# A fifth chunk place, two swapped places and an earlier third row block in a linear-attention and Fourier mixing kernel

## The chip, the cores and the metric

The kernel runs on one core of one Trainium2 chip. The metric is the device time of one execution in microseconds (us). The kernel before takes 724.97 us, the median of three runs (724.33 to 727.36).

A core has a matrix engine (TensorE, PE in the profile, with its weight loads as PEld), a vector engine (VectorE, DVE), an engine for pointwise functions (ScalarE, ACT), and GpSimd (POOL) and SyncE (SP), which here only issue DMAs once the start is over. Each engine works through its own queue in order. They meet through semaphores. TensorE writes to banks of an accumulation memory (PSUM). Everything else lies in the on-chip memory (SBUF) or in the chip's main memory (HBM).

## The reference

The input x is 2048 x 576. The result is a gated mix of a linear attention block with 32 heads and a two-dimensional Fourier layer:

```
g = sigmoid((x * gate_w).sum(-1))
q, k, v = x @ wqkv                      # each 2048 x 576, 32 heads of 18
phi(t)  = where(t > 0, t + 1, exp(t)) + 1e-6
kv  = phi(k)^T v per head;  z = sum of phi(k) over the rows
o   = (phi(q) kv) / (phi(q) z + 1e-6)
a   = o @ wo
b   = dft_seq_re @ (x @ dft_hid_re^T) - dft_seq_im @ (x @ dft_hid_im^T)
result = g * a + (1 - g) * b
```

All is float32. The kernel keeps that precision by splitting each operand of a matmul into a high part and a low part (high on ScalarE as a rounding copy, low on VectorE as the difference), and by three matmuls for each product: high x high, high x low, low x high.

## The kernel before

The stages come one after the other, and the time of each is in the profile below.

**The k stage.** k' = phi(x W_k) is made, 16 blocks of 128 rows, and kept split on the chip (`pk`). While that runs, POOL fetches transposed blocks of x for later, two 128-row blocks (a "pair") at a time. A pair is turned into seven combined blocks ("forms"), because the products x W_q and x W_hidden are later done by a scheme of seven products for four. The class `Left` holds such a pair: its loads (line 366), sums (199), high parts (179) and low parts (189), and its stores to HBM (`xm<-xb`, line 398). Pairs 2, 3, 4 and 5 take turns in two places of SBUF of 14,336 bytes per partition, one from offset 15104 of the slot area to 29440, one from 29440 to 43776. Pair k+2 waits until pair k's stores have landed.

**The k'^T x stage** (line 752). Instead of k'^T v the kernel makes G = x^T k', and then, for each 128 rows of G, multiplies with W_v (`kv_step`). x comes as 20 chunks of 128 x 512, which I number 0 to 19: four for each of the five column blocks c. Chunk n is used in step n: 24 matmuls, or 16 in the last four steps, whose column block is narrow. A chunk is loaded by SP (`craw<-in_xg_dram`, line 599), split by ScalarE (`c<-craw`, 179) and VectorE (`c<-craw,c`, 189), and then read by TensorE. The chunks lie in a ring of four places (`cs_ring`). `xg_load` is called once per step after that step's matmuls, so the load of chunk n+4 goes into the place of chunk n; SP holds it until the matmuls of step n are done. `xg_next` splits chunk n+2 in step n.

In the same steps lies work for the q stage: the forms of pairs 6 and 8 (pair 8 stands for the odd columns of all pairs), pair 5's stores, and W_q. W_q is prepared by `right_here` in three pieces: two pieces of 128 rows (generators `wq_pieces[0]` and `[1]`, called `a` and `b` in the table `turn`) and the remaining 64 rows, laid out as 96 (`wq_pieces[2]`, `c`). Each piece is two loads by POOL (line 469), four sums on VectorE (199), one high part on ScalarE and one or two low parts on VectorE. The table `turn` says in which step a generator is moved one stage on. The second piece lies at offset 16128 to 32256 of the slot area, so it overlaps both places of the pairs. The third has its result at 32256 to 40320 and its raw data from 40320 to 48384, so it overlaps only the upper place.

**The q stage** (line 928). q' = phi(x W_q) by the seven products, in 56 slots, `q_slot`, four groups of two pairs: (6, 2), (3, 4), (0, 5), (7, 1). Some pairs' forms come from HBM (`xf<-xm`), some are made on the spot (`xb`). In the table `plan` each slot is given further work: the product of kv with W_o (`build_m`, then moved by DMA to other partitions with `move_m`, `mw<-mf`, and split with `split_m`), the forms of pairs 7, 0 and 1 (`left[k]`), the norms, and the first transposes of q' (`transposed(0)`).

**The rest.** o @ W_o (line 209 with `mw`), the hidden Fourier transforms (1133) and the two sequence transforms (1289), from 198 us on.

What sets the order: TensorE's order in the q stage, and SP's everywhere, is the order of the program text. In the k'^T x stage a scheduler orders TensorE's and POOL's instructions by a simulated timeline and by priority, so that TensorE's queue there has some matmuls of a later chunk in front of the rest of an earlier one. `pace()` fixes ScalarE's and VectorE's order to the program's.

The scratch for the exponentials, `es` (three places of 1184 bytes at `Y_AT`), is used in the k stage and in the q stage, and lies unused in between.

Of the kernel before, what the change touches and what calls it, by code (L numbers as in the profile page):

```python
# [136 lines left out]
def kernel(  # L137
# [373 lines left out]
    def go(gen, n=1):  # L511
        for _ in range(n):
            next(gen, None)
# [46 lines left out]
    for h in range(2):  # L560
        ps = [bank()[:, :QH[h]] for _ in range(FT)]
        parts = wkt.split(h, KC)
        for c, (raw, hi, lo) in enumerate(first):
            if h == 0:
                if c == 0:
                    nc.vector.tensor_copy(out=hi, in_=raw)
                else:
                    done.append(hi_of(hi, raw))
                lo_of(lo, raw, hi)
            next(parts)  # L570
            passes = ((hi, c), (lo, c), (hi, 5 + c))[:3 if c < KC else 2]
            for n, (x, j) in enumerate(passes):
                for i in range(FT):
                    nc.tensor.matmul(ps[i], x[:, i * P:(i + 1) * P], wkt.row(h, j),
                                     start=(c == 0 and n == 0), stop=(c == KC and n == 1))
        if h == 0:
            banks = ps
            lefts.append(Left(2, SLOT_AT + 15104, done[-1]).make())
    for i in range(FT):
        k_feature(i, 0, banks[i])  # L580
    split_next()
# [1 line left out]
    for i in range(FT):  # L583
        k_feature(i, 1, ps[i])
        if i < 2:
# [2 lines left out]
    wq_w, wq_pieces = right_here(wq, wq_rest, (T_AT + 112896, SLOT_AT + 16128),  # L588
                                 SLOT_AT + 32256, SLOT_AT + 40320)
    cs_ring = Ring(C_AT, 2 * CU * P * 4, 4)  # L590
    xg_order = [(c, q) for c in range(5) for q in range(NCU)]
    xg_raw, xg_split = [], []

# [19 lines left out]
    for i in range(FT, NT):  # L613
        xs = split.pop(0)
        k_half(i, 0, xs)
        if i < NT - 2:
            split_next()
        left_part()
        if i >= NT - 2:
            xg_next()  # L620
        held = pending[:]
        pending.clear()
        k_half(i, 1, xs)
        for f in held:
            f()
        if i in (10, 12, 14):
            add(zacc, zacc if i > 10 else acc[0], acc[i // 2 - 4])
        if i == 5:
            go(wq_pieces[0])
        if 8 <= i < 12:  # L630
            xg_load()
        if i < NT - 1:
            load_next()
        if i == FT:
            load_next()
        for k, j in ((3, 4), (4, 9), (5, 13)):
            if i == j:
                lefts.append(Left(k, SLOT_AT + 15104 + k % 2 * 14336, done[-1]).make())
    tick()
    nc.scalar.activation(gate, gate, AF.Exp, scale=-1.0)  # L640
    nc.vector.tensor_scalar(gate, gate, 1.0, None, op0=ALU.add)
# [77 lines left out]
    def load_two(*places):  # L719
        for p, o in places:  # L720
            forms[p] = at(o, [P, 7, 2, 2 * P], R, "xf")
        for a, b in ((2, 4), (0, 2), (4, 7)):
# [1 line left out]
                nc.sync.dma_start(out=forms[p].bitcast(F)[:, a:b], in_=xforms[p][:, a:b])  # L724

    turns = dict(p=rest_forms(), a=wq_pieces[0], b=wq_pieces[1], c=wq_pieces[2], x=left_of(6, False))
    turn = {4: "p", 5: "p", 6: "p", 7: "p", 8: "pap", 9: "pa", 10: "pax", 11: "pxpaa",
            12: "pbbxb", 13: "xcb", 14: "cc", 15: "xc", 17: "b"}

    plan = {  # L730
        2: [lambda: begin_left(NP, ACC_AT)],
        6: [z_chain, lambda: begin_left(6, ACC_AT + 22784)],
        8: [z_sum],
        12: [lambda: load_wo(2)],
        14: [lambda: load_forms(2, ACC_AT + 8448, nc.gpsimd), lambda: load_wo(3)],
# [7 lines left out]
    for c in range(5):  # L743
        ps = [bank(), bank()]
        passes = FULL if c < KC else FULL[:2]
        for q in range(NCU):
# [26 lines left out]
            del spaced[:n]  # L773
            if step == 9:
                go(wq_pieces[1])
                go(wq_pieces[2])
            for k in turn.get(step, ""):
                go(turns[k])
            step += 1
# [242 lines left out]
        44: [lambda: here[7].store(slice(0, 4), done[-1]),  # L1022
             lambda: here[7].store(slice(4, 7), done[-1])],
    }
    for k, what in ((7, (10, 11, 13, 15, 20)), (0, (13, 15, 18, 20, 20)),
                    (1, (31, 35, 36, 36, 36)), (None, (25, 27, 30, 41, 43, 45, 48, 48, 49, 52)),
                    ("m", (28, 30, 28, 35, 33))):
        for n, j in enumerate(what):
            f = norm if k is None else m_parts[n] if k == "m" else lambda k=k: go(left[k])
            plan.setdefault(j, []).append(f)  # L1030
# [10 lines left out]
    with tc.manual_schedule(engines={mybir.EngineType.PE}):  # L1041
        for k, (n, s, q) in enumerate(slots):
            q_slot(n, s, q)
            for f in plan.get(k, ()):
                f()
            if k == 49:
                nxt = transposed(0)
    while feats or dves:
        if feats:
# [465 lines left out]
```

## Time and profile before

| what | us |
|---|---|
| median of the runs (3) | 724.97 |
| profiled execution | 726.96 |
| its span, first to last instruction | 725.2 |
| TensorE busy | 716.6 |
| VectorE busy | 595.3 |
| ScalarE busy | 331.2 |

By stages, from the view of busy time in windows: from 53 to 135 us, where the k stage ends and the k'^T x stage runs, TensorE is busy all but some 3 us; from 135 to 198 (the q stage) all but about 0.6; and from 198 to 544 it has no gap in that view. How to read it: a matmul's end is modelled, so the start of the next one tells better than its end whether TensorE stood still. A row of the timeline gives start, duration, engine, line, operation, what is written from what, how many instructions are merged in the row, and in brackets the idle time before the first of them and what ended it. A row of waits gives the total, the number and the longest. In rows of DMAs the last number is the median from issue to landing. A releaser is inferred; where several semaphores are waited for, the named one is the last by the profile.

### The profile page before, as it was taken

The numbers are of one execution on the slowest core, as the hardware profiler recorded it, in microseconds if no ns is written. First come the engines' busy times: TensorE is split into PE (matmuls) and PEld (weight loads), VectorE is DVE, ScalarE is ACT, GpSimd is POOL, SyncE is SP. The second block draws the span as 40 slices with busy tenths as digits, with TensorE's granted clock in tenths as the row PEclk, the third lists the DMA queues.
The fourth block names the chain that finished last, engine by engine and source line by source line (L and its number), as shares of the span: only waits on it lengthen the run. The fifth ranks groups of instructions, "written<-read, shape, count | busy, mean of one in ns | idle before, by whom it ended". The sixth has DMA issues, their size and how long they took to land.

```text
span 725.2 us, 13800 instructions
## 1 busy us (share of the span) xinstructions
PE 716.6 (99%) x5390; PEld 714.2 (98%) x5390; DVE 595.3 (82%) x993; ACT 331.2 (46%) x507; POOL 78.7 (11%) x141
## 2 busy tenths in 40 slices
PE   9999999999999999999999999999999999999998
PEld 9999999999999999999999999999999999999997
DVE  5799987477999748989899989857889988788884
ACT  6898445478545634453334333323535322232321
POOL 1122431123252100000000000000000000000000
PEclk9999999999999999999999999999999999999999
DMA  7385789999279648444476666889963544454440
GB/s 256 117 254 188 249 277 323 328 318 271 105 274 393 247 159 320 131 163 139 153 234 203 231 224 197 281 318 398 372 210 132 172 147 127 131 171 154 153 153 33
DMA packets 54093, 157.85 MB, mean 218 GB/s; under 512 B 6884, under 2 KB 9348, under 8 KB 54028
## 3 DMA queue, kind: packets, MB, share of 16 engines
q1 hardware_dynamic: 42524, 117.23, 48.3%
q0 software_dynamic: 11216, 39.32, 15.5%
q8 instruction: 43, 0.70, 0.4%
q10 hardware_dynamic: 288, 0.41, 0.2%
q14 instruction: 22, 0.18, 0.1%
HBM read 117.80 MB, written 36.49 MB: 213 GB/s over the span
## 4 chain that ended last, share of the span: by engine, by line
PE 75%; DVE 5%; DMA 3%; ACT 2%; issue 1%; POOL 0%; DVEq 0%; POOLq 0%; ACTq 0%
PE bank L1289 49%; PE bank L1133 14%; PE bank L209 8%; PE bank L928 2%; DMA craw<-in_xg_dram 1%; PE bank L839 1%; DMA wraw<-in_wq_rest_dram 1%; DVE xb L189 1%; ACT xb L179 1%; DMA xb<-in_xq_dram 1%; DVE sum L199 1%; PE bank L752 1%; DVE acc L938 0%; DVE den L808 0%; DVE xb L199 0%
## 5 line engine op out<-in xcount | busy, mean ns | idle before, releaser
L1289 PE MATMUL bank<-fh,c 128*128 128x288 f32 x1792 | 355.8, 295 | 0.0
L1289 PEld LDWEIGHTS bank<-fh,c 128*128 128x128 f32 x1792 | 285.9, 188 | 0.2 <-DVE c L189 0.2
L1289 PE MATMUL bank<-fl,c 128*128 128x288 f32 x896 | 262.8, 293 | 0.0
L179 ACT ACTIVATE c<-craw 128x1792 fp32r<-128x1792 f32 (+1 forms) x84 | 121.4, 1447 | 185.5 <-DVE craw L199 162.5
L1289 PEld LDWEIGHTS bank<-fl,c 128*128 128x128 f32 x896 | 168.7, 188 | 0.0
L189 DVE TENSOR_TENSOR c<-craw,c 128x1792 fp32r<-128x1792 f32 (+4 forms) x86 | 141.9, 1653 | 4.7 <-ACT c L179 4.5
L199 DVE TENSOR_TENSOR craw<-craw 128x256 f32<-128x256 f32 (+1 forms) x192 | 98.1, 512 | 21.6 <-DMA craw<-in_ci_dram 10.8
L1133 PE MATMUL bank<-wf,xf 128*128 128x288 f32 x630 | 98.5, 296 | 0.0
L1133 PEld LDWEIGHTS bank<-wf,xf 128*128 128x128 f32 x630 | 90.0, 189 | 0.0
L752 PE MATMUL bank<-pk,c 128*128 128x288 f32 x448 | 62.4, 297 | 3.2 <-DVE c L189 1.8
L752 PEld LDWEIGHTS bank<-pk,c 128*128 128x128 f32 x448 | 60.2, 188 | 4.1 <-DVE c L189 2.5
L209 PE MATMUL bank<-mw,qs 128*128 128x288 f32 x448 | 63.2, 297 | 0.1
L209 PEld LDWEIGHTS bank<-mw,qs 128*128 128x128 f32 x448 | 59.9, 188 | 0.6 <-ACT qs L179 0.4
L209 PE MATMUL bank<-wd,xs 128*128 128x288 f32 (+1 forms) x336 | 44.7, 295 | 0.0
L209 PEld LDWEIGHTS bank<-wd,xs 128*128 128x128 f32 x336 | 44.6, 188 | 0.0
L199 DVE TENSOR_TENSOR ys<-bank,ys 128x288 f32<-128x288 f32 x63 | 28.8, 456 | 17.4 <-PE bank L1289 14.2
L189 DVE TENSOR_TENSOR fl<-fl,fh 128x864 fp32r<-128x864 f32 (+1 forms) x32 | 34.6, 1092 | 7.0 <-ACT fh L179 5.8
L179 ACT ACTIVATE fh<-fl 128x864 fp32r<-128x864 f32 (+1 forms) x32 | 29.8, 950 | 16.3 <-DVE fl L199 16.3
L398 POOL DMA_DIRECT2D xm<-xb x56 | 30.3, 547 | 29.0 <-ACT sum L969 8.4
L1133 PE MATMUL bank<-wf,xr 96*128 96x288 f32 x112 | 33.3, 298 | 0.0
L1311 ACT ACTIVATE ys<-bank 128x288 f32<-128x288 f32 x16 | 6.6, 413 | 56.3 <-PE bank L1289 56.3
L199 DVE TENSOR_TENSOR ys<-ys,bank 128x288 f32<-128x288 f32 x47 | 21.1, 449 | 13.3 <-PE bank L1289 12.7
(133 smaller groups left out, 805.1 us busy)
## 6 DMA issues: line engine op xcount, KB each, us to landing
xf<-xm SPq DMA_DIRECT2D x49, 512.0 KB, 9.2
craw<-in_cr_dram SPq DMA_DIRECT2D x32, 512.0 KB, 3.6
craw<-in_ci_dram SPq DMA_DIRECT2D x32, 512.0 KB, 3.8
xm<-xb POOLq DMA_DIRECT2D x56, 256.0 KB, 4.7
xr<-xr SPq DMA_DIRECT2D x21, 448.0 KB, 8.7
craw<-in_xg_dram SPq DMA_DIRECT2D x20, 256.0 KB, 5.7
att<-acc POOLq DMA_DIRECT2D x16, 288.0 KB, 3.2
row<-att SPq DMA_DIRECT2D x16, 288.0 KB, 4.3
```

The costliest lines, as they stand in the source:

```text
L179: return nc.scalar.activation(dst, src, AF.Copy, bias=bias)
L189: nc.vector.tensor_tensor(out=dst, in0=src, in1=hi, op=ALU.subtract)
L199: nc.vector.tensor_tensor(out=dst, in0=a, in1=b, op=op)
L209: nc.tensor.matmul(ps, a, b, start=(n == 0), stop=(n == len(pairs) - 1))
L398: ins = nc.gpsimd.dma_start(out=xforms[self.k][:, f], in_=self.c.bitcast(F)[:, f])
L752: nc.tensor.matmul(ps[h][:, :HALF], t[:, a, k], pk[s][:, b, half(h)], start=(s == 0 and n == 0), stop=(s == NT - 1 and n == len(passes) - 1))
L839: nc.tensor.transpose(banks[c // KC][:, (c % KC) * P:(c % KC + 1) * P], a, ident)
L928: nc.tensor.matmul(ps, a, b, start=(start and n == 0), stop=(stop and n == len(ops) - 1), skip_group_check=True)
L1133: nc.tensor.matmul(ps, a, b, start=(start and n == 0), stop=(n == len(ops) - 1), skip_group_check=True)
L1289: nc.tensor.matmul(ps[q], c[x][:, l, k], factors[p](y, f), start=(p == 0 and i == 0), stop=(p == NP - 1 and i == 2))
L1311: nc.scalar.activation(c11, ps[1], AF.Copy)
```

## The change

Four things are changed together. First, `cs_ring` gets a fifth place at `Y_AT`, on the scratch of the exponentials: chunk n+4 now goes to the place of chunk n-1. Second, the two places of the pairs are swapped: pairs 2 and 4 now lie in the upper place, 3 and 5 in the lower. Third, W_q's third piece is loaded in step 7 (it was step 9, after the second piece) and its sums, high part and low part come in steps 10 to 12, ahead of the second piece's. Fourth, some work has other slots in the q stage: the last low part of pair 0 goes from slot 20 to 23 and that of pair 1 from 36 to 38, `split_m(0, 0)` from 28 to 24, `split_m(1, 1)` from 35 to 34, and the first transposes from after slot 49 to after slot 50.

```diff
-            lefts.append(Left(2, SLOT_AT + 15104, done[-1]).make())
+            lefts.append(Left(2, SLOT_AT + 29440, done[-1]).make())
...
     cs_ring = Ring(C_AT, 2 * CU * P * 4, 4)
+    cs_ring.at.append(Y_AT)
...
-                lefts.append(Left(k, SLOT_AT + 15104 + k % 2 * 14336, done[-1]).make())
+                lefts.append(Left(k, SLOT_AT + 29440 - k % 2 * 14336, done[-1]).make())
...
-    turn = {4: "p", 5: "p", 6: "p", 7: "p", 8: "pap", 9: "pa", 10: "pax", 11: "pxpaa",
-            12: "pbbxb", 13: "xcb", 14: "cc", 15: "xc", 17: "b"}
+    turn = {4: "p", 5: "p", 6: "p", 7: "p", 8: "pap", 9: "pa", 10: "paxc", 11: "pxpaac",
+            12: "pcxcb", 13: "xbb", 14: "b", 15: "x", 17: "b"}
...
+        7: [lambda: go(wq_pieces[2])],
...
                 go(wq_pieces[1])
-                go(wq_pieces[2])
...
-    for k, what in ((7, (10, 11, 13, 15, 20)), (0, (13, 15, 18, 20, 20)),
-                    (1, (31, 35, 36, 36, 36)), (None, (25, 27, 30, 41, 43, 45, 48, 48, 49, 52)),
-                    ("m", (28, 30, 28, 35, 33))):
+    for k, what in ((7, (10, 11, 13, 15, 20)), (0, (13, 15, 18, 20, 23)),
+                    (1, (31, 35, 36, 36, 38)), (None, (25, 27, 30, 41, 43, 45, 48, 48, 49, 52)),
+                    ("m", (24, 30, 28, 34, 33))):
...
-            if k == 49:
+            if k == 50:
                 nxt = transposed(0)
```

The order of SP's queue is the same in both kernels, and TensorE's too but for the transposes. What moves on the other engines is shown at three places. Numbers behind names only tell buffers apart.

POOL's queue in steps 6 to 9 of the k'^T x stage, before. `xm_110` are pair 4's stores, `xb_1274` pair 6's loads, `xm_111` pair 5's stores, and the loads of line 469 are W_q's second and third rows:

```order
L398 DMA xm_110<-xb_691 128x512 x7
L366 DMA xb_1274<-in_xq_dram 128x2x256 x2
L398 DMA xm_111<-xb_894 128x512 x7
L469 DMA wraw_1411<-in_wq_dram 128x3x288
L469 DMA wraw_1411<-in_wq_dram 128x288
L469 DMA wraw_1415<-in_wq_rest_dram 96x864
L469 DMA wraw_1415<-in_wq_rest_dram 96x288
```

The same place after the change:

```order
L398 DMA xm_110<-xb_691 128x512 x7
L469 DMA wraw_1313<-in_wq_rest_dram 96x864
L469 DMA wraw_1313<-in_wq_rest_dram 96x288
L366 DMA xb_1274<-in_xq_dram 128x2x256 x2
L398 DMA xm_111<-xb_894 128x512 x7
L469 DMA wraw_1415<-in_wq_dram 128x3x288
L469 DMA wraw_1415<-in_wq_dram 128x288
```

The third rows' two loads have moved past pair 6's loads and pair 5's stores; the second rows' loads are still behind those stores.

VectorE's queue from chunk 13's low part (`c_1394`) to chunk 15's (`c_1482`), before. `c_1449` is chunk 14, `wraw_1411` and `wb_1412` are W_q's second rows, `wraw_1415` the third, `xb_1275` is pair 6:

```order
L189 TENSOR_TENSOR c_1394<-craw_1392,c_1394 128x512
L189 TENSOR_TENSOR plain_1406<-wraw_1407,plain_1406 128x576
L189 TENSOR_TENSOR gt_1491<-bank,gt_1491 128x288 x2
L199 TENSOR_TENSOR wraw_1411<-wraw_1411 128x288 x4
L189 TENSOR_TENSOR c_1449<-craw_1447,c_1449 128x512
L189 TENSOR_TENSOR xb_1275<-xb_1274,xb_1275 128x4x256
L199 TENSOR_TENSOR wraw_1415<-wraw_1415 96x288 x2
L189 TENSOR_TENSOR wb_1412<-wraw_1411,wb_1412 128x4x288
L189 TENSOR_TENSOR c_1482<-craw_1480,c_1482 128x512
```

After the change, where `c_1398` is chunk 13, `c_1484` chunk 15, `wraw_1415` now the second rows and `wb_1314` the third:

```order
L189 TENSOR_TENSOR c_1398<-craw_1396,c_1398 128x512
L189 TENSOR_TENSOR plain_1410<-wraw_1411,plain_1410 128x576
L189 TENSOR_TENSOR gt_1495<-bank,gt_1495 128x288 x2
L189 TENSOR_TENSOR wb_1314<-wraw_1313,wb_1314 32x2016
L199 TENSOR_TENSOR wraw_1415<-wraw_1415 128x288 x2
L189 TENSOR_TENSOR c_1449<-craw_1447,c_1449 128x512
L189 TENSOR_TENSOR xb_1275<-xb_1274,xb_1275 128x4x256
L199 TENSOR_TENSOR wraw_1415<-wraw_1415 128x288 x2
L189 TENSOR_TENSOR c_1484<-craw_1482,c_1484 128x512
```

Ahead of chunk 14's low part stand two sums on the second rows instead of four, and the second rows' low part has gone from before chunk 15's low part to behind it; the third rows' low part has come to the front.

ScalarE's queue in slots 22 to 28 of the q stage, before. `e` are exponentials of q', `sum_1959` and `sum_1960` copies from the banks, and `mw_2241` the high parts of the product of kv with W_o:

```order
L937 ACTIVATE e_2171<-sum_1967,less_88 128x288
L937 ACTIVATE e_2183<-sum_1968,less_88 128x288
L941 ACTIVATE e_2193<-bank 128x288
L942 ACTIVATE e_2193<-e_2193 128x288
L967 ACTIVATE sum_1959<-bank 128x288
L937 ACTIVATE e_2214<-sum_1965,less_88 128x288
L967 ACTIVATE sum_1960<-bank 128x288
L179 ACTIVATE mw_2241<-mw_2085 128x1152 x2
```

After the change (`mw_2185` is the same product):

```order
L938 ACTIVATE e_2170<-sum_1967,less_88 128x288
L938 ACTIVATE e_2183<-sum_1968,less_88 128x288
L179 ACTIVATE mw_2185<-mw_2085 128x1152
L942 ACTIVATE e_2195<-bank 128x288
L943 ACTIVATE e_2195<-e_2195 128x288
L968 ACTIVATE sum_1959<-bank 128x288
L938 ACTIVATE e_2216<-sum_1965,less_88 128x288
L968 ACTIVATE sum_1960<-bank 128x288
L179 ACTIVATE mw_2185<-mw_2085 128x1152
```

One of the two high parts has moved ahead of five other instructions.

## The prediction

> **What bounds the kernel now.** I read the page first, then what TensorE's weight loads waited for, then TensorE's rows in the stage that the change touches.
>
> ```profile
> span 725.2 us, 13800 instructions
> PE 716.6 (99%) x5390; PEld 714.2 (98%) x5390; DVE 595.3 (82%) x993; ACT 331.2 (46%) x507; POOL 78.7 (11%) x141
> ...
> PEld bank L752 <- DVE c L189: 2.5, 3, 1.2
> PEld bank L752 <- ACT c L179: 1.6, 1, 1.6
> ...
> PEld bank L928 <- DVE xb L189: 0.6, 1, 0.6
> ```
>
> TensorE is busy for 99% of the span, and the change takes no matmul away. So all that can be won is idle time of TensorE: 4.1 us (2.5 + 1.6) at line 752, the stage k'^T x, and 0.6 us in the q stage (L928). Beyond that there is next to nothing to gain.
>
> ```profile
> 99.40 0.64 PE L752 MATMUL bank<-pk,c 128*128 128x288 f32 x3
> 101.37 12.51 PE L752 MATMUL bank<-pk,c 128*128 128x288 f32 x92 [1.34 <-ACT c L179]
> ...
> 114.69 0.77 PE L752 MATMUL bank<-pk,c 128*128 128x288 f32 x4
> 115.89 3.45 PE L752 MATMUL bank<-pk,c 128*128 128x288 f32 x24 [0.43 <-DVE c L189]
> 119.75 5.11 PE L752 MATMUL bank<-pk,c 128*128 128x288 f32 x36 [0.40 <-DVE c L189]
> ...
> 128.62 2.37 PE L752 MATMUL bank<-pk,c 128*128 128x288 f32 x16
> 132.00 2.44 PE L752 MATMUL bank<-pk,c 128*128 128x288 f32 x16 [1.01 <-DVE c L189]
> ```
>
> These are TensorE's rows around the four stalls. Ninety-two matmuls in 12.51 us start 0.134 us apart. After the three at 99.40 the next was due at 99.80 and came at 101.37: stall 1, 1.57 us. In the same way stall 2 is 0.66 (due 115.23), stall 3 is 0.64 (due 119.11), and stall 4 is 1.24 (due 130.76). The sum is 4.11, as the weight loads have it.
>
> **Stalls 1 and 4: the fifth place.** They come from late chunks.
>
> ```profile
> SPq L599 <- PE bank L752: 38.9, 15, 5.0
> ...
> 88.38 7.02 SPq L599 DMA_DIRECT2D craw<-in_xg_dram  x3
> 118.85 0.33 SPq L599 DMA_DIRECT2D craw<-in_xg_dram  x1
> 122.71 8.06 DMA craw<-in_xg_dram
> ...
> 97.01 0.63 ACT L179 ACTIVATE c<-craw 128x512 fp32r<-128x512 f32 x1 [0.76 <-DMA craw<-in_xg_dram]
> 100.69 0.63 ACT L179 ACTIVATE c<-craw 128x512 fp32r<-128x512 f32 x1 [3.04 <-DMA craw<-in_xg_dram]
> 130.85 0.63 ACT L179 ACTIVATE c<-craw 128x512 fp32r<-128x512 f32 x1 [5.60 <-DMA craw<-in_xg_dram]
> ```
>
> The first row says that 15 chunk loads waited for TensorE: with four places, chunk n+4 is loaded when step n is done. With five it is loaded when step n-1 is done, one step (24 x 0.134 = 3.2 us) sooner, where nothing else holds SP.
> Stall 1 waits for chunk 12's high part, 100.69 on ScalarE. Its load is the last of the three from 88.38 on, at 88.38 + 7.02 - 0.33 = 95.07, and it landed near 100.6. One step sooner is 91.9, so it lands near 97.5. ScalarE has made chunk 11's part at 97.01 + 0.63 and is free, so the part is there near 98.3, before 99.80. Stall 1 goes, with 1.5 us to spare: -1.57. Next late would be chunk 13, which no matmul needs for another three steps.
> Stall 4 waits for chunk 19, issued at 122.71 and landed 8.06 later. One step sooner is the time of the row at 118.85, less what stalls 1 and 3 give back by then (about 1.6): 117.3. Landed after the same 8.06 it is there at 125.4, split about 1.2 later on ScalarE and VectorE, and due at 130.76 - 2.2 = 128.6. Stall 4 goes too, with 2 us to spare: -1.24.
> The fifth place lies on the scratch of the exponentials in the k and q stages. Chunk 4 waits there for the k stage's last features, which end before step 0 does; chunk 19 is used up before the q stage's first features are due: 0.
>
> **Stalls 2 and 3: W_q.** These two come from VectorE's queue.
>
> ```profile
> 113.42 1.81 DVE L199 TENSOR_TENSOR wraw<-wraw 128x288 f32<-128x288 f32 x4 [4.46 <-DMA wraw<-in_wq_rest_dram]
> 115.16 0.68 DVE L189 TENSOR_TENSOR c<-craw,c 128x512 fp32r<-128x512 f32 x1
> 115.76 1.22 DVE L189 TENSOR_TENSOR xb<-xb,xb 128x1024 fp32r<-128x1024 f32 x1
> 116.89 0.93 DVE L199 TENSOR_TENSOR wraw<-wraw 96x288 f32<-96x288 f32 x2
> ...
> 119.02 0.68 DVE L189 TENSOR_TENSOR c<-craw,c 128x512 fp32r<-128x512 f32 x1
> ...
> 122.51 2.25 DVE L189 TENSOR_TENSOR wb<-wraw,wb 32x2016 fp32r<-32x2016 f32 x1 [0.75 <-ACT wb L179]
> ...
> 120.59 1.89 ACT L179 ACTIVATE wb<-wraw 96x2016 fp32r<-96x2016 f32 x1 [2.13 <-DVE wraw L199]
> ...
> 93.76 1.07 POOL L398 DMA_DIRECT2D xm<-xb  x2 [0.41 <-ACT zb L659]
> 98.06 1.08 POOL L398 DMA_DIRECT2D xm<-xb  x2 [3.22 <-ACT c L179]
> 105.33 1.31 POOL L469 DMA_DIRECT2D wraw<-in_wq_dram  x2 [6.20 <-issue]
> ...
> wraw<-in_wq_dram POOLq DMA_DIRECT2D x1, 432.0 KB, 7.2
> ```
>
> VectorE stands for 4.46 us before the sums on W_q's second rows, and chunk 14's low part (115.16 to 115.84) is queued behind all four. The row names the third rows; by the program it is the second that are summed there, issued at 105.33 and 7.2 us on the way, the small piece behind them a little more.
> After the change two sums stand ahead of chunk 14 instead of four, which saves 0.9, but TensorE comes 1.57 sooner, at 113.66. The load itself can hardly go earlier: POOL starts it when pair 5's stores have landed, and their last two go after chunk 11's high part. That part's 0.76 us of waiting for its chunk ends, so all of it moves by about 0.7: sums from 112.7, low part at 112.7 + 0.93 + 0.66 = 114.3. Stall 2 is then 0.65 and stays: 0. Bounds: unmoved load, 115.0, stall 1.35 (+0.7); a load that lands another 0.65 sooner, since the third rows no longer follow it, no stall (-0.66).
> Stall 3: between the two chunks' low parts stood xb, two sums, a low part of W_q; now only xb and two sums: 1.1 + 0.9 + 0.65 = 2.7 us after chunk 14, where TensorE needs it 24 x 0.134 = 3.2 after. It goes: -0.64. ScalarE must not be later than that; its high part of W_q's second rows (1.9 us) now stands behind chunk 15's.
> The third rows, two DMAs, now go about 89, ahead of pair 6's loads on POOL, which the swap allows: they overlap the place of pair 4 alone. Their work is covered by VectorE's wait. VectorE began it at 113.42 - 4.46 = 108.96, so 107.4 with stall 1 gone; ScalarE's high part (1.89) and then VectorE's low part (2.25) end near 111.7, a microsecond ahead of 112.7: 0. Were that cover gone, each microsecond would go into stall 2. For the swap itself, two pairs each still share a place: 0.
>
> **The q stage.** No gain is booked. The pieces that move are two low parts of 0.95 us on VectorE, one of the two W-products' high parts on ScalarE, and a transpose one product later.
>
> ```profile
> 162.21 2.06 ACT L937 ACTIVATE e<-sum,less 128x288 f32<-128x288 f32 x4 [2.06 <-DVE sum L199]
> 165.95 2.21 ACT L179 ACTIVATE mw<-mw 128x1152 fp32r<-128x1152 f32 x2
> 165.54 1.45 POOL L366 DMA_DIRECT2D xb<-in_xq_dram  x2 [10.79 <-ACT sum L967]
> ...
> 185.00:198.00 13.00, 12.85 (x99) 12.56 (x98) 12.74 (x30) 6.97 (x18) 3.57 (x7) 1.00 0.36 142
> ```
>
> From 185 to 198 VectorE (third pair of numbers) is busy 12.74 of 13 us beside a TensorE busy 12.85. Both are full there, so TensorE ends the stage when VectorE does, and VectorE's work stays the same. The chain that leads there starts at exponentials that wait 2.06 us for VectorE's sums; they release pair 1's load at 165.54. Pair 0's low part (0.95) moves behind those sums, and one high part (2.21 / 2 = 1.1) moves ahead of the release: +0.15, taken as 0. Bounds: -0.6 (L928's wait goes) to +1.1 (the low part was no help).
>
> **The sum.** -1.57 + 0 - 0.64 - 1.24 = -3.45. The profiled execution took 726.96 (span 725.2, 1.72 around it): 723.5. The median shown is 724.97, 1.99 less than that. If those 1.99 lie outside the stalls, the new median is 724.97 - 3.45 = 721.5. If the median run simply has that much less of the stalls, only 1.5 of the 3.45 is there to win: 723.5. I take the middle, 722.5.
>
> **Two rules of the Trainium skill.** The page "DMA: Bandwidth & Descriptors", section "Anatomy of one DMA — SWDGE (gpsimd) path", gives a GpSimd DMA a fixed 2.0 us plus bytes by 436 GB/s; for 432 KB that is an estimate of 3.0 us, stall 2 would vanish and the sum be -4.1. The 7.2 us of this trace disagrees. The same page, section "Issuing engines are not separate DMA queues", says that DMAs of all issuers share the same 16 engines, so starting them otherwise wins only issue time; that speaks against this change and would lead to rival C.
>
> **Rivals.**
>
> ```profile
> 125.00:135.00 10.00, 8.99 (x69) 8.76 (x69) 5.13 (x10) 2.25 (x6) 0.11 (x1) 1.00 0.96 360
> ...
> 152.88 1.25 SPq L712 DMA_DIRECT2D xr<-xr  x2
> xr<-xr SPq DMA_DIRECT2D x2, 448.0 KB, 8.7
> mw<-mf SPq DMA_DIRECT2D x1, 252.0 KB, 10.0
> ...
> 88.72 1.46 POOL L366 DMA_DIRECT2D xb<-in_xq_dram  x2 [7.15 <-ACT c L179]
> 76.89 0.72 POOL L372 DMA_DIRECT2D xb<-in_xq_dram  x1 [1.81 <-issue]
> ```
>
> A, all goes: stall 2 and the q waits end as well. 724.97 - 4.1 - 0.6 = 720.3, or some 721 if the median has less to lose. For it: the small piece only needs 0.65.
> B, given back in the q stage: ScalarE's first high part of the W-product, moved from slot 28 to 24, needs a 9 KB piece that SP issues behind two loads of xr. The second of these goes about 153.8 and takes 8.7: 162.5. ScalarE comes at 164.27 - 0.95 = 163.3, so in the old timing nothing waits; but if TensorE comes 3.45 sooner and these DMAs don't, it waits 2.6, and pair 1's load, VectorE's chain and TensorE with it. 724.97 - 3.45 + 2.7 = 724.2; with the next piece's 10.0 us, up to 726.6. Against it: these DMAs are released by TensorE's own progress, so they should move along.
> C, it doesn't do what it says: the DMA engines are 0.96 busy from 125 to 135. If chunk 19 lands at 130.8 whenever it is issued, TensorE still resumes at 132.00, and every stall won before is lost there: 725.0. Against it: chunk 19's load was among the last that went, and it now goes 5 us sooner.
> D, slower: POOL works in order. The third rows' loads go where the loads of 88.72 went, and wait for pair 4's stores; pair 6's loads, pair 5's seven stores and the second rows' load stand behind them. POOL has also waited 1.81 us at 76.89 for nothing but its own queue. If two more DMAs in flight put off the stores by one landing (4 us), the second rows are 4 us later and stall 2 is 0.65 + 4.1: 725.6. From 3.45 us of delay on it is slower than before, from 7.1 by over 0.5%: 728.6. For it: stall 2 has no slack at all. Against it: the stores at 93.76 went 4 us before the last two at 98.06, which wait for ScalarE, not for POOL.
>
> **Chances.** Forecast 0.57 (its own range 721.4 to 723.6), A 0.16, B 0.12, C 0.08, D 0.07. A difference under 0.5% (3.6 us) is about what a measurement of this kernel can't tell from none. Faster than 721.35 takes A and the edge of the forecast: 0.19. Slower than 728.6 is half of D and a little of B: 0.05. Within: 0.76. The range goes from 720.7 (most of A) to 725.5 (B's middle, C, D's edge).
>
> **What would show it.** Right: TensorE's waits at the chunk stage's matmuls fall from 4.1 to about 0.7 us, ScalarE no longer waits 3.04 and 5.60 us for chunks 12 and 19, VectorE still waits for W_q's second rows near 112, and the q stage's rows are shifted by 3 to 4 us. Wrong: a wait before the matmuls on pair 1 (L928) that is longer than 0.6 us (B), chunk 19 landing near 130 again (C), W_q's second rows issued later than 105.3 (D).

## The result and the profile after

| | median us | executions | ratio to the kernel before, 95% interval |
|---|---|---|---|
| before | 725.39 | 10 | |
| after | 722.94 | 10 | 0.9953, [0.9941, 0.9966] |

The three executions shown ahead (median 724.97) are among the ten. The median of the kernel after is 2.45 us lower, 0.34%; the ratio in the table, which is not that of the two medians, lies 0.47% below 1, and its interval excludes 1. So the kernel after is faster, by about as much as the prediction's bound of 0.5%; the median forecast was 722.5. The profiled execution of the kernel after took 724.75, the slowest of its ten (the fastest took 720.50), against 726.96 before.

The page of the kernel after, its first lines:

```profile
span 723.0 us, 13795 instructions
PE 715.7 (99%) x5390; PEld 714.7 (99%) x5390; DVE 594.8 (82%) x993; ACT 331.1 (46%) x507; POOL 79.0 (11%) x141
```

What TensorE's weight loads waited for in the kernel after (total us, times, longest). Line 754 is the stage k'^T x, which was 752 before; 929 is the q stage, which was 928:

```profile
PEld bank L754 <- DVE c L189: 1.5, 1, 1.5
PEld bank L929 <- DVE xb L189: 1.4, 1, 1.4
```

Of 4.1 us at the chunks' matmuls 1.5 is left, in one piece. Before the matmuls on pair 1 there is now 1.4 where 0.6 stood. TensorE's rows in the chunk stage of the kernel after:

```profile
100.05 12.87 PE L754 MATMUL bank<-pk,c 128*128 128x288 f32 x95
...
113.73 0.76 PE L754 MATMUL bank<-pk,c 128*128 128x288 f32 x4
115.81 8.29 PE L754 MATMUL bank<-pk,c 128*128 128x288 f32 x60 [1.31 <-DVE c L189]
124.72 2.33 PE L754 MATMUL bank<-pk,c 128*128 128x288 f32 x16
127.85 4.53 PE L754 MATMUL bank<-pk,c 128*128 128x288 f32 x32
```

Stall 1 is gone: the 95 matmuls from 100.05 on hold the three that stood alone at 99.40 and the 92 behind the stall. Stalls 3 and 4 are gone too: sixty matmuls and then thirty-two run through where rows broke off at 119.75 and 132.00. Stall 2 has grown. The fourth matmul from 113.73 on starts at 114.20, the next was due 0.134 later and came at 115.81: 1.47 us. Counted like this, from one start to the next less 0.134, the four stalls of the kernel before are 1.50, 0.60, 0.57 and 1.17, together 3.8; the prediction's 4.11 takes its due times from the starts of rows. All stalls from here on are counted from start to start, so stall 2 went from 0.60 to 1.47.

All times of this execution lie 0.64 us late from 16 us on. Its first loads are not the reason: TensorE began its first x products at 5.07 us here and at 5.25 before. But from 5.45 to 6.90 they start 0.24 us apart here, and about 0.134 apart before. The trace's record of TensorE's granted clock, the share of full speed that it is given, has its first entry at full clock at 6.95 us here and at 4.83 before; 0.24 us is also the spacing under a granted clock of 0.50 further below (no_q_slots). So the clock rose later in this execution. In a second execution of the same kernel (after_again) it rose at 4.21, so this differs from one execution to the next. By 16 us the profiled executions of this study lie up to 0.8 us apart.

ScalarE's rows for chunks 12 and 19 in the kernel after:

```profile
97.94 0.63 ACT L179 ACTIVATE c<-craw 128x512 fp32r<-128x512 f32 x1 [0.53 <-DMA craw<-in_xg_dram]
...
126.16 0.63 ACT L179 ACTIVATE c<-craw 128x512 fp32r<-128x512 f32 x1 [2.70 <-DMA craw<-in_xg_dram]
```

They stood at 100.69 and 130.85. Both chunks are now early enough.

Stall 2, first on POOL's queue and then on VectorE, in the kernel after:

```profile
97.83 1.07 POOL L398 DMA_DIRECT2D xm<-xb  x2 [1.31 <-ACT c L179]
106.06 1.31 POOL L469 DMA_DIRECT2D wraw<-in_wq_dram  x2 [7.16 <-DMA xm<-xb]
```

```profile
114.19 0.95 DVE L199 TENSOR_TENSOR wraw<-wraw 128x288 f32<-128x288 f32 x2 [2.09 <-DMA wraw<-in_wq_dram]
115.06 0.69 DVE L189 TENSOR_TENSOR c<-craw,c 128x512 fp32r<-128x512 f32 x1
```

Pair 5's last two stores go at 97.83, so 0.87 sooner than before once the 0.64 is taken off. The load that waits for their landing goes at 106.06, which is 105.42 less the 0.64: where it went before (105.33). The stores took longer. This is the DMA view of the stretch from 97 to 107.5 us, with the median us from issue to landing, of the kernel before and of the kernel after:

```profile
xm<-xb POOLq DMA_DIRECT2D x2, 256.0 KB, 5.5
```

```profile
xm<-xb POOLq DMA_DIRECT2D x2, 256.0 KB, 6.5
wraw<-in_wq_dram POOLq DMA_DIRECT2D x1, 432.0 KB, 7.3
```

And the stretch from 95 to 105, of before and of after; the last three numbers are the granted clock, the busy share of the DMA engines and the GB/s:

```profile
95.00:105.00 10.00, 8.66 (x67) 8.43 (x67) 8.54 (x17) 4.13 (x6) 1.08 (x2) 1.00 0.91 327
```

```profile
95.00:105.00 10.00, 10.00 (x79) 10.00 (x79) 9.83 (x20) 4.08 (x5) 2.35 (x5) 1.00 1.00 382
```

The share rose from 0.91 to 1.00. Whether fuller engines make these stores slow is tested below.

The q stage of the kernel after, VectorE's rows and TensorE's:

```profile
170.38 0.76 DVE L199 TENSOR_TENSOR xb<-xb 128x256 f32<-128x256 f32 x2 [2.19 <-DMA xb<-in_xq_dram]
...
175.22 1.23 DVE L189 TENSOR_TENSOR xb<-xb,xb 128x1024 fp32r<-128x1024 f32 x1 [1.27 <-ACT xb L179]
```

```profile
174.91 0.43 PE L929 MATMUL bank<-wb,xb 128*128 128x288 f32 x2
176.50 0.80 PE L929 MATMUL bank<-wb,xb 128*128 128x288 f32 x4 [1.16 <-DVE xb L189]
```

VectorE waits for pair 1's load, whose second half landed at 170.29, and TensorE resumes 6.2 us after the landing. This wait is 1.32 us, against 0.54 before. Two small gaps that the kernel before had, 0.18 at 162 and 0.29 at 197, are gone.

### The profile page after: what moved, and what is told of

It is laid out like the page before. It is cut to its first block, busy times and chain, and to the rows that moved or that the text cites. A ratio compares the mean times of both kernels' runs of the same rounds, so it can differ in the third digit from the quotient of the medians.

```text
span 723.0 us, 13795 instructions
## 1 busy us (share of the span) xinstructions
PE 715.7 (99%) x5390; PEld 714.7 (99%) x5390; DVE 594.8 (82%) x993; ACT 331.1 (46%) x507; POOL 79.0 (11%) x141
## 4 chain that ended last, share of the span: by engine, by line
PE 92%; DMA 3%; DVE 2%; ACT 1%; issue 0%; POOL 0%; DVEq 0%; POOLq 0%
PE bank L1290 49%; PE bank L209 15%; PE bank L1134 15%; PE bank L754 6%; PE bank L929 4%; PE bank L574 2%; PE bank L840 1%; DMA wraw<-in_wq_dram 1%; DMA xm<-xb 1%; DMA xb<-in_xq_dram 1%; ACT xb L179 1%; DVE xb L189 1%; PE bank L235 1%; DVE xb L199 0%; DVE sum L199 0%
```

## The experiments

The theory after this comparison: the stalls lie one behind another, and the middle one hangs on a load whose time TensorE does not set. Pair 5's last store lands; 1 us later the load of W_q's second rows goes; some 7 us later it lands; then VectorE's sums run, and chunk 14's low part behind them. Taking stall 1 away brings TensorE sooner to that same landing. The first rival is that the four terms add up one by one, as the prediction had them.

**The fifth place alone (fifth_only).** On the kernel before:

```diff
     cs_ring = Ring(C_AT, 2 * CU * P * 4, 4)
+    cs_ring.at.append(Y_AT)
```

> The kernel before with the fifth place alone. Theory (stalls are coupled: chunk 14's low part waits in VectorE's queue behind the four sums on W_q's rows, and those wait for a load whose landing does not follow TensorE): stalls 1 and 4 go (-1.57, -1.24), but TensorE only comes 1.57 us sooner to stall 2, which grows from 0.66 to about 2.2; stall 3 stays at 0.64. Net -1.2 us, 724.2. Rival (the terms simply add, as the prediction had them, and the load of the second rows moves 0.7 with the stores): stall 2 is about 1.5, net -1.9, 723.5; with stall 2 unchanged, net -2.8, 722.6.

Median 724.61, ratio 0.9985, [0.9974, 0.9995]: 1.0 us under the kernel before on the same chip (725.61). TensorE's rows:

```profile
100.12 12.88 PE L753 MATMUL bank<-pk,c 128*128 128x288 f32 x95
...
115.45 3.71 PE L753 MATMUL bank<-pk,c 128*128 128x288 f32 x26 [1.13 <-DVE c L189]
119.31 5.10 PE L753 MATMUL bank<-pk,c 128*128 128x288 f32 x36 [0.15 <-DVE c L189]
```

Stalls 1 and 4 are gone by the fifth place alone. Stall 2 is 1.28 and stall 3 0.32, where the theory had 2.2 and 0.64. In this execution the load went at 104.40, 0.9 sooner than before, and its start lies late like that of the kernel after, so the load did move with the stores, as the rival had it; its 1.5 is nearer to this stall 2 than the theory's 2.2. The median sides with the theory (1.0 where it had 1.2), and the rival's 1.9 lies at the edge of the interval (0.9974 is 1.9 us). What is shown is the coupling: stall 2 doubled, from 0.60 to 1.28, although its load came sooner. How much is given back differs with the landing.

**W_q's order alone (wq_only).** The kernel after without the line above, and with the q stage's slots as before.

> The kernel after without the fifth place and with the q stage's slots as before: W_q's third rows ahead of its second, and the two places swapped. Theory: stalls 1 and 4 stay (1.57, 1.24). Chunk 14's low part stands behind two sums instead of four, 0.9 us sooner, so stall 2 (0.66) and stall 3 (0.64) go: -1.3, 724.1. Rival (two more loads among pair 5's stores put those off, and with them the second rows' load, by 0.7 us or more): stall 2 stays at 0.5 or more and stall 1 grows, net -0.6 or less, 724.8 or more.

Median 725.50, ratio 0.9998, [0.9987, 1.0010]: nothing. TensorE's row behind stall 1:

```profile
102.10 12.50 PE L753 MATMUL bank<-pk,c 128*128 128x288 f32 x92 [1.87 <-ACT c L179]
```

Stall 1 is 2.03 instead of 1.50: chunk 12's load took 6.07 instead of 5.53. Stall 3 is gone, so that term belongs to VectorE's order. Stall 2 is 0.59, as before, although two sums fewer stand ahead. These are ScalarE's rows and then VectorE's:

```profile
110.18 0.63 ACT L179 ACTIVATE c<-craw 128x512 fp32r<-128x512 f32 x1 [0.97 <-DMA craw<-in_xg_dram]
110.80 1.89 ACT L179 ACTIVATE wb<-wraw 96x2016 fp32r<-96x2016 f32 x1
```

```profile
112.72 2.25 DVE L189 TENSOR_TENSOR wb<-wraw,wb 32x2016 fp32r<-32x2016 f32 x1 [3.02 <-ACT wb L179]
115.00 0.95 DVE L199 TENSOR_TENSOR wraw<-wraw 128x288 f32<-128x288 f32 x2
115.86 0.68 DVE L189 TENSOR_TENSOR c<-craw,c 128x512 fp32r<-128x512 f32 x1
```

The load of W_q's second rows was issued 0.65 later than before (105.98), but its small piece landed at 113.13, where before it landed at 113.11. VectorE did not wait for it here: until 114.97 it made the low part of the third rows, which waited for ScalarE's high part, and that stood behind chunk 14, which landed only at 110.10. With the fifth place chunk 14 landed at 107.17, and the same low part was done at 112.11. So the rival's two signs are there, but stall 2 has another cause than the rival's: without the fifth place the third rows are no longer covered. In this one execution stall 4 is absent as well, without the fifth place: chunk 19, issued at 122.74 as before, was there 6.9 us later instead of 8.1. The profile thus shows less idle than the median makes of it, and how much the order gains by itself in the median is not settled beyond the interval (0.9 us gained to 0.7 lost).

By medians the two parts give 1.0 and 0.1 us alone, and 2.4 together (next run). The intervals do not exclude that they add. The rows show why they may be worth more together: W_q's order takes two sums out of the queue that the fifth place leaves TensorE waiting at, and the fifth place brings chunk 14 early enough for the third rows to be out of the way.

**Without the q stage's slots (no_q_slots).** The kernel after with these lines as in the kernel before:

```diff
-    for k, what in ((7, (10, 11, 13, 15, 20)), (0, (13, 15, 18, 20, 23)),
-                    (1, (31, 35, 36, 36, 38)), (None, (25, 27, 30, 41, 43, 45, 48, 48, 49, 52)),
-                    ("m", (24, 30, 28, 34, 33))):
+    for k, what in ((7, (10, 11, 13, 15, 20)), (0, (13, 15, 18, 20, 20)),
+                    (1, (31, 35, 36, 36, 36)), (None, (25, 27, 30, 41, 43, 45, 48, 48, 49, 52)),
+                    ("m", (28, 30, 28, 35, 33))):
...
-            if k == 50:
+            if k == 49:
```

> The kernel after with the q stage's slots as in the kernel before. Theory (the longer wait before the matmuls on pair 1, 1.3 us against 0.5, comes of pair 1's load, not of the slots): the wait stays near 1.3, and the two small gaps at the products before it (0.2) and at the end of the stage (0.3) come back: 723.2 to 723.4. Rival (the slots have made the wait longer): it falls to 0.5 or less, 722.2 to 722.6.

Median 723.25, ratio 0.9974, [0.9961, 0.9987], where the theory had 723.2 to 723.4. The two small gaps are back (0.18 and 0.29). But the wait before pair 1 is 0.27, as the rival had it. So the slots take the small gaps away, and whether they lengthen the other wait is looked at with the runs below. The chunk stage of this execution showed something else:

```profile
116.97 9.57 PE L754 MATMUL bank<-pk,c 128*128 128x288 f32 x60 [2.36 <-DVE c L189]
```

```profile
117.60:118.00 0.40, 0.40 (x3) 0.40 (x3) 0.40 (x2) 0.00 (x0) 0.00 (x0) 0.50 0.86 307
```

Here the last store landed at 105.89 and stall 2 was 2.5 us. TensorE's granted clock was 0.50 from 116.44, half a microsecond before it resumed, to 119.86, and the sixty matmuls took 9.57 us where the kernel after took 8.29.

**The sums later (sums_later, sums_later2).** On the kernel after, so that chunk 14's low part is queued ahead of the sums on W_q's second rows; the load stays:

```diff
-            12: "pcxcb", 13: "xbb", 14: "b", 15: "x", 17: "b"}
+            12: "pcxc", 13: "xbbb", 14: "b", 15: "x", 17: "b"}
```

> The kernel after with the sums on W_q's second rows one step later, so behind chunk 14's low part in VectorE's queue; the load stays where it is. Theory (stall 2 is nothing but chunk 14's low part queued behind sums that wait for the load): stall 2 (1.47 us) goes, chunk 15's low part is still ahead of its need (117.4): 721.4 to 721.6, 1.4 us under the kernel after. Rival (the wait moves on to chunk 15, whose low part now stands behind the same sums, the two of xb and the load's landing): a stall of 0.5 to 1.4 us before chunk 15, 722.0 to 722.9.

> The kernel after with the sums on W_q's second rows one step later, as before, now beside the kernel after on one chip. Theory (the later sums take stall 2 away whenever the load is late): no wait before chunk 14, median 0.8 to 1.2 us under the kernel after, and a smaller spread (about 2 us from fastest to slowest where the kernel after has 4). Rival (it only moves the wait on to chunk 15): no difference, within 0.4 us.

Medians 722.05 (0.9952, [0.9940, 0.9963]) and 722.21 (0.9955, [0.9941, 0.9968]). No stall is left in the chunk stage of either execution. VectorE's rows in the second:

```profile
112.32 0.69 DVE L189 TENSOR_TENSOR c<-craw,c 128x512 fp32r<-128x512 f32 x1
112.93 1.22 DVE L189 TENSOR_TENSOR xb<-xb,xb 128x1024 fp32r<-128x1024 f32 x1
114.07 1.80 DVE L199 TENSOR_TENSOR wraw<-wraw 128x288 f32<-128x288 f32 x4
115.79 0.68 DVE L189 TENSOR_TENSOR c<-craw,c 128x512 fp32r<-128x512 f32 x1
```

The load's small piece landed at 113.64 here; in a run below (pair1_only), with the sums in their old place, it landed at 113.66, and stall 2 was 1.15. So the mechanism is shown: with the fifth place, stall 2 is chunk 14's low part queued behind sums that wait for the load, and it does not move on to chunk 15. What it is worth in the median is less than I expected: 0.15 against the kernel after on the same chip (722.36), so the rival's "within 0.4" is what the times say. The spread was 3 us (721.38 to 724.43) in the second run, for a reason of its own: a wait of 1.67 before pair 1 in that execution.

**The kernel after once more (after_again).**

> The kernel after once more, for a second profiled execution beside the next three. Theory (stall 2 follows the landing of pair 5's last store: in six profiles the load of W_q's second rows went 0.95 to 0.99 us after it, and landed 6.4 to 7.7 us later): the last store lands anywhere from 102.6 to 106, and stall 2 ends 1.7 us after the small piece of the load has landed, between 113.9 (none) and 117; the wait before the matmuls on pair 1 was one execution's landing and is 0.1 to 0.5 this time. Median 722.9. Rival: both waits (1.5 and 1.3) belong to the kernel and are there again.

Median 722.36, ratio 0.9960, [0.9944, 0.9976]. The profiled execution took 722.45, and its chunk stage has no stall 2:

```profile
113.50 8.81 PE L754 MATMUL bank<-pk,c 128*128 128x288 f32 x64
```

The last store landed at 103.25 instead of 105.08, the load's small piece at 112.28 instead of 114.07. In all thirteen usable profiles of this study, whatever the kernel, the load went 0.95 to 0.99 us after the last store had landed. In the three with the third rows first and a stall 2 above 1 us (after, pair1_only, no_q_slots), TensorE resumed 1.73 to 1.74 us after the small piece. So stall 2 is not a fixed cost of the kernel after: it was 1.47 in one execution and nothing in the other, with the landing. The expectation failed on pair 1: the wait there was 1.02 this time, so it came in both executions.

**The xr stores later (xr_later, xr_later2).** The six stores of the last pairs' third rows (448 KB each) are taken out of steps 8 to 12 of the kernel after, and put into 12 and 13:

```diff
-    turn = {4: "p", 5: "p", 6: "p", 7: "p", 8: "pap", 9: "pa", 10: "paxc", 11: "pxpaac",
-            12: "pcxcb", 13: "xbb", 14: "b", 15: "x", 17: "b"}
+    turn = {4: "p", 5: "p", 6: "p", 7: "p", 8: "pa", 9: "a", 10: "axc", 11: "xaac",
+            12: "cxcbppp", 13: "xbbppp", 14: "b", 15: "x", 17: "b"}
```

> The kernel after with the six stores of the last pairs' third rows (xr, 448 KB each) held back from steps 8 to 12 to steps 12 and 13; nothing else moves. Theory (pair 5's stores are slow because the 16 DMA engines are full from 95 to 105): with some 2 MB less to move there the last store lands by 103, the load of W_q's second rows goes by 104 and lands by 111.5, and stall 2 is 0.5 or less; 721.8 to 722.4 if chunks 18 and 19, which then meet the six stores, are still in time, up to 723.5 if not. Rival (the stores are slow for a reason of POOL's queue): the last store lands at 104 to 106 as before, stall 2 stays near 1.5.

The profiled execution took 1414 us, with matmuls of 467 ns instead of 295, and says nothing on the stalls. The median of the other seven is 722.48, ratio 0.9961, [0.9942, 0.9979].

> The kernel after with the six xr stores of 448 KB held back to steps 12 and 13, a second time, since the profile of the first shows TensorE at half its pace from end to end and tells nothing of the stalls. Theory (pair 5's stores are slow because the DMA engines are full from 95 to 105): the last store takes under 5.5 us instead of 5.1 to 7.4, lands by 103.5, and the load of W_q's second rows goes 1 us behind it; no stall 2 above 0.5. Rival (POOL's own queue makes them slow): 5.1 to 7.4 us as in the five profiles with the stores in their place. Time by either within 0.5 us of the kernel after.

Median 722.65, ratio 0.9954, [0.9940, 0.9968]. The DMA view from 97 to 107.5, and the stretch from 95 to 105:

```profile
xm<-xb POOLq DMA_DIRECT2D x2, 256.0 KB, 3.9
wraw<-in_wq_dram POOLq DMA_DIRECT2D x1, 432.0 KB, 4.5
```

```profile
95.00:105.00 10.00, 10.00 (x79) 10.00 (x78) 9.83 (x20) 4.44 (x6) 3.00 (x6) 1.00 0.79 265
```

The engines are 0.79 busy from 95 to 105, and 0.66 while the load of 432 KB is on its way. The two stores took 3.9 us and the load 4.5. In the twelve other usable profiles the stores took 4.4 to 6.1 us where the engines were 0.91 to 0.97 busy from 95 to 105 and 6.0 to 7.1 where they were 0.98 to 1.00, and the load 6.4 to 7.7 with engines 0.81 to 0.99 busy on its way. Stall 2 is gone: the load is there 3.6 us before VectorE comes to its sums. POOL's queue issues the same instructions in the same order, so the rival falls: what else the DMA engines move sets how long these stores and the load take. Not shown is that the change itself made the stores slower: with the third rows first they took 4.4 to 7.1 us in nine profiles, with the old order 5.0 to 5.7 in three. The time is that of the kernel after all the same. The six stores now meet the loads behind them, and a product of the q stage on forms from HBM waits 0.7 us at 142.6; that this is where the gain went is not shown.

**Pair 1's load sooner (pair1_only, and with the sums later: pair1_sooner, both_again).** On the kernel after, or on the one with the sums later:

```diff
     def begin_left(k, o):
-        here[k] = Left(k, o, done[-1])
+        here[k] = Left(k, o, done[-1 if k != 1 else -2])
```

> The sums later, and the load of pair 1 released by the exponential before the one that releases it now. Theory (TensorE is done with the place 2.4 us before the load goes; ScalarE's later exponential alone holds it): the load goes 1.5 to 2.3 us sooner relative to TensorE and no wait before the matmuls on pair 1 is left; since this wait is 0.1 to 0.3 in most executions, the median falls by 0 to 0.3 against the sums later alone. Rival (the load is held by TensorE or by POOL): it goes when it went, no difference.

> The kernel after with pair 1's load released by the exponential before, the sums on W_q's second rows left where the kernel after has them. Theory (the wait before the matmuls on pair 1 is the larger loss in the median execution; the later sums took 0.2 us or nothing off it): the load goes some 2 us sooner, no wait there, 721.1 to 721.7, within 0.5 of the version with both. Rival (stall 2 is there in half the executions and costs as much): 721.8 to 722.2, half-way between the kernel after and the version with both, and a spread of 3 us.

> The sums later and pair 1's load released sooner, a second time. Theory: 720.9 to 721.4, all executions within 1 us of each other, no wait of TensorE over 0.3 us from 60 to 200 us; 1.3 us under the kernel after and 4.4 under the kernel before. Rival (the first measurement caught six quiet executions): 722 with a spread of 3 us.

| | median us | ratio, 95% interval |
|---|---|---|
| pair1_only | 721.73 | 0.9955, [0.9941, 0.9969] |
| with the sums later (pair1_sooner) | 721.07 | 0.9943, [0.9926, 0.9960] |
| the same once more (both_again) | 721.46 | 0.9944, [0.9926, 0.9961] |

POOL's row in both_again:

```profile
160.24 1.45 POOL L366 DMA_DIRECT2D xb<-in_xq_dram  x2 [9.04 <-ACT e L938]
```

The load goes at 160.24 where it went at 161.7 to 163.5 with the release of the kernel after. Its second half takes 6.2 to 6.5 us, no less than before, and in none of the three profiles is a wait left before pair 1. So the exponential held the load, not TensorE. I had expected 0 to 0.3 us of it; the median fell by 1.1 (722.21 to 721.07) beside the sums later on the same chip. By medians pair1_only lies 0.6 to 1.2 under the kernel after, but on another chip, and its ratio (0.9955) is no lower than the kernel after's (0.9953 and 0.9960), so that alone it gains is not settled. It still has stall 2 (1.15). With both edits TensorE has no wait over 0.3 us from 60 to 205 us in either execution, and all twelve times lie between 720.68 and 722.28. The second median lies a little over the theory's 721.4, the spread over its 1 us. This is the fastest version found, 4.0 to 4.5 us under the kernel before; its interval overlaps the kernel after's.

For the size of this wait, the profiles stand so. In the four where the load decided (before, after, after_again, sums_later2), TensorE resumed 6.2 us after the second half had landed. With the old slots that half took 4.0 to 5.7 us in five profiles (waits of 0.27, and 0.54 once); with the new slots and the old release 4.2 to 6.6 in five (waits of 0, 0.16, 1.02, 1.32, 1.67). The ranges overlap, so whether the new slots make the load itself slower stays open. They do send it off later: with the old slots it was issued 12.03 to 12.05 us before TensorE was due at pair 1 in all five profiles, with the new ones 11.71 to 11.72 in four and 11.90 in one, and with the sooner release 13.52 in all three.

**The kernel before once more (before_again).**

> The kernel before once more, for a second profiled execution: the profile that the prediction was made from (726.96) lay 1.6 us above the median. Theory (the landing of loads differs from one execution to the next by up to 3 us, the stalls with it): in an execution near 725.4 the stalls at the chunks' matmuls add up to 2.5 to 3.5 us instead of 4.1, stall 1 (released by TensorE's own progress) is there again, stalls 2 and 4 (each behind a load that takes 7 to 8 us) are where the difference lies. Rival: the four stalls are the same 4.1, and the difference lies outside them.

Median 725.64, ratio 0.9992, [0.9980, 1.0004]. Its four stalls are 1.21, 0.52, 0.57 and 1.07, together 3.4 instead of 3.8, and the wait before pair 1 is 0.27 instead of 0.54. Yet this execution took 727.03. Neither side is right: stall 1 varied most of the four, and the rest lies elsewhere. TensorE ran 0.30 us late at 16 us, and later, in a sequence transform, it waited twice for VectorE's low part of a chunk, at 435.4 and 452.4 us. All weight-load waits from 200 us to the end, in this execution and then in the first one of the kernel before:

```profile
PEld bank L1289 <- DVE c L189: 0.7, 2, 0.4
```

```profile
PEld bank L1289 <- DVE c L189: 0.2, 1, 0.2
```

Matmul for matmul, this execution is 0.57 us ahead of the first at 198 us and 0.08 behind it at the end: the late waits gave back 0.64.

## Why the prediction was right, and where it was not

- **The median: right, in part by luck.** 722.5 was forecast; 722.94 and 722.36 were measured. The step that made it so was to take the middle between 721.5 and 723.5, since the profiled execution was slower than the median. That is a choice between two cases and no mechanism, and its reason (a median execution has less of the stalls) is not borne out: before_again took 727.03 with less of them. The profile itself fell by 2.2 instead of 3.45, and by 2.85 without the later start of 0.64, which the rise of the clock made.
- **Stall 1: right.** Chunk 12 was to be issued at 91.9, landed near 97.5 and be split near 98.3; it was issued at 92.77 and split by 98.57, in an execution that lies 0.64 late as a whole. fifth_only shows that the fifth place does it.
- **Stall 4: right.** Gone in fifth_only too. Chunk 19's load went at 118.81 instead of 117.3, since stall 2 gave back part of what was won and the execution lay 0.64 late. wq_only shows that this stall also hangs on one landing.
- **Stall 3: right.** Gone in every profile with the new order on VectorE, and still 0.32 and 0.57 with the old one (fifth_only, before_again).
- **Stall 2: mechanism right, size wrong.** The step that failed is "all of it moves by about 0.7": the stores did go sooner, but took 6.5 us instead of 5.5 in engines that were 1.00 busy, and the load went where it had gone before. The term was booked as no change, at 0.65; the profile gave 1.47, a little over the upper bound (1.35), and the second profile none, the lower bound. One value was the wrong form for this term: it is what a landing leaves, and in the nine profiles with the third rows first and the xr stores in their place the last store landed anywhere from 102.6 to 105.9.
- **The third rows' cover: right.** VectorE's low part of them ran from 109.86 to 112.11 (less 0.64: 109.2 to 111.5, where 111.7 was forecast), ahead of the sums. That this cover hangs on the fifth place was missed: in wq_only, without it, the same low part ran to 114.97 and made stall 2, as the prediction said of a cover that is gone.
- **The q stage: booked at 0, measured +0.3.** Two gaps went (0.47), which the prediction had not counted among what can be won, and the wait before pair 1 grew by 0.78. The sum lies within the bounds (-0.6 to +1.1). Of the 0.78, the load's later issue is 0.34 (the step "+0.15, taken as 0"), and its second half took 0.43 longer (6.09 instead of 5.66), which no term had. The sign named for rival B, a wait over 0.6 before pair 1, came, but not its mechanism: ScalarE's high part of the W-product waited for nothing at 161.05.
- **Rival A.** Its half on stall 2 came in one of the two profiles of the kernel after; the wait in the q stage stayed in both.
- **Rival C and the rule behind it.** Chunk 19 did come sooner, so C fell. But the rule of the Trainium skill that it went with (page "DMA: Bandwidth & Descriptors", section "Issuing engines are not separate DMA queues") bears on one stall earlier: xr_later2 shows that loads and stores in the same engines hold each other up, whoever issues them, since there SP's stores were held back and POOL's landed sooner. The estimate of 3.0 us for 432 KB, from the same page of the Trainium skill (section "Anatomy of one DMA — SWDGE (gpsimd) path"), was not reached in any profile: 6.4 to 7.7 us with the engines 0.81 to 0.99 busy on the way, 4.5 with 0.66.
- **Rival D.** In the profile of the kernel after the stores landed later than the prediction had them, by one microsecond instead of four. They were not issued later, so the delay lies in their transfer and not in POOL's order.

## What to carry to other kernels

Stalls that follow one another need not add: before you sum them, ask for each whether its end moves with the engine that waits, or with a load that lands when it lands. Where the DMA engines are nearly full, the time of a load hangs on what else they move, so it is safer to queue the work that waits for a load behind the work that the bounding engine needs next than to hurry the load. A term that hangs on one landing should be read in two profiles, and given as a range.

## What the runs showed of the hardware that was not expected

- Idle time can cost more than itself. In no_q_slots, after 2.36 us without a matmul, the granted clock was 0.50 for 3.41 us, and sixty matmuls took 1.3 us longer. After the 1.87 us in wq_only and the 1.3 us in the kernel after it stayed at 1.00. The length of the gap may not be all that counts: in all thirteen usable profiles the granted clock changes only at multiples of 3.413 us from its first rise. In the one such span of no_q_slots that ends where the clock fell, TensorE was busy 1.58 us; around the stalls of wq_only and the kernel after it was busy 2.12 and 2.10 us of such a span. The Trainium skill, page "TensorE: Matmul & The Clock Gate", section "What's actually happening", gives an idle window of about 3.4 us for this; here a span of that length was enough in which TensorE was busy for nearly half. The span before the fall and the one after it, with TensorE's busy time and matmuls, the granted clock, and the share and GB/s of the DMA engines (a transfer counts where it starts, so the share can pass 1):

```profile
113.03:116.44 3.41, 1.58 (x15) 1.00 1.06 383
116.44:119.85 3.41, 2.88 (x12) 0.50 0.81 227
```

- Such falls are part of the spread. In eleven executions of the kernel before, of those measured beside the experiments and in before_again, the mean granted clock was 0.997 or 0.998. They took 726.8 to 728.1 us; the median of the others was 725.5.
- The same load of 432 KB took 4.5 us with the engines 0.66 busy while it was on its way, and 6.4 to 7.7 with 0.81 to 0.99.
- Two executions of the fastest version lay 0.9 us apart (721.39 and 722.28) with no wait of TensorE above 0.3 us from 60 to 205 us in either. Of that, 0.14 arose by 8 us, and some 0.77 at 430.6 and 447.6 us, where TensorE waited for VectorE's low part of a chunk in one of them and not in the other. The slower one's weight-load waits from 200 us on:

```profile
PEld bank L1290 <- DVE c L189: 0.6, 2, 0.3
```
